# Taking the four batches of a gated recurrence side by side, chunk by chunk

## The chip, the cores and the metric

The kernel runs on one core of one Trainium2 chip, as one launch. The metric is the device time of that launch in microseconds (us), the median of several runs. A profile of one execution is given beside it; its span runs from the first to the last instruction.

## The reference

Two blocks follow each other. The first is a gated linear recurrence (HGRN2) for 4 batches, 8 heads, 768 tokens and 48 channels per head; the second is a feed-forward network on its output, 3072 tokens of 384 channels. Cut to what matters:

```python
f = 1.0 / (1.0 + np.exp(-f_logit))               # (4, 8, 768, 48)
state = np.zeros((B, H, D, D))
for t in range(S):
    state = f[:, :, t, :, None] * state + np.einsum('bhd,bhe->bhde', k[:, :, t], v[:, :, t])
    y[:, :, t] = np.einsum('bhd,bhde->bhe', q[:, :, t], state)
x = y.transpose(0, 2, 1, 3).reshape(B * S, H * D)   # (3072, 384)
h = ((x @ w1) * (x @ w2)) @ w3                      # w1, w2: (384, 1024), w3: (1024, 1024)
out = h @ w_out                                     # (1024, 384)
```

Each batch has its own state, which starts at zero. The four weight matrices arrive as 64-bit floats and are turned into 32-bit ones on the chip.

## The kernel before, in words

**Chunks.** The 4 x 768 tokens are cut into `NU` = 24 chunks of `C` = 128 tokens. Chunk `u` belongs to batch `u // 6`, so chunks 0 to 5 are the first batch in order of time, 6 to 11 the second, and so on. A chunk "opens" when it is the first of its batch (0, 6, 12, 18; no state comes in) and "closes" when it is the last (5, 11, 17, 23; no state goes out). Heads are handled in pairs: a tile has 112 rows, 48 for an even head, 48 for an odd one from row 64 on, and 4 x 128 columns.

**Work of a chunk.** `front` (L477) loads the logits, k, q and v through SyncE's DMA queue (L492, L475), lets ScalarE apply the sigmoid (`gates`, L518) and VectorE run two scans over the gates (`forward`, L526; `backward`, L548); the running products scale q (L542) and k (L556), and the last product of each head is kept in `lasts` (L531). `turning` transposes the scaled k on TensorE (L593) and copies it (L727). `pairs` makes the products of k and q (L569 for chunks 0 and 1, L579 for the others), ScalarE copies them (L700, L703) and GpSimd zeroes what lies above the diagonal (L709). `values` (L653) multiplies the masked products with v, `from_state` (L672) adds q times the state, and `update` (L686) makes the chunk's own contribution to the state. ScalarE writes the result (L845). For chunks 0 and 1 it is brought into the token layout by matmuls (`moved`, L874, and L879); for the others by two DMA writes to DRAM and a DMA read back (L866, L869).

**Two kinds of chunk.** Chunks 0 and 1 (`u < NPE`) are taken whole: `first_values` (L607), four matmuls against the state of the chunk before in a block-diagonal copy (L613; the copy is made by `blocks`, L834), `first_update` (L625) and the state in L822, or L824 and L825. From chunk 2 on a chunk is taken in two halves of 64 tokens: `middle` (L749) makes a state at token 64 (L757 where the chunk opens, else L759 adds the state that comes in) and the state at the end (L762). `state` (L815) multiplies the end state by a gain (L818); the gain is made on GpSimd (`gains`, L809) from `lasts` of this chunk and the first gate of the next one, so it waits for the next chunk's sigmoid.

From chunk 4 on, `visit` (L787) puts the values of chunk `u`, and the pairs and update of chunk `u+1`, into one run of matmuls on TensorE.

**Feed-forward.** Four chunks make a block of 512 tokens (6 blocks). w1 and w2 come in four pieces A, B, C, D (`fetch`, L1378: load L1396, then L1400 on ScalarE and L1415, L1419, L1425 on VectorE); w3 and w_out are folded into one matrix (L1464). Block 0 is multiplied plainly (`part`, L919), blocks 1 and 2 with seven products in place of eight (`seven`, L972), blocks 3 to 5 with a larger scheme of that kind (`many`, L1120). Three of them share the helper `three` at L897. Late in the run ScalarE also looks over the weights' ranges (L1536, L1540), in gaps of its plan.

**Order.** Nothing is scheduled by hand. Each step is a task of a `Plan` (L129) with an engine, an estimated cost, dependencies and a priority; the planner takes at each step the task that can start first by its estimates, then the one with the smaller priority, and the instructions of every engine stand in that order. `need(u)` (L454) is a chunk's due time, 0 to 3 for chunks 0 to 3 and 60 + 14.5 (u - 4) after. `EARLY` (L83) fixes the order of VectorE's early work: chunks 0, 1, 2, 3, then the weight pieces A, C, B, D. Up to the planned time `FULL` = 130, planned gaps of TensorE are filled with matmuls that compute nothing (`idle`, L395, at L399):

```python
    if t["eng"] == "PE" and t["at"] < FULL:
        n = int((t["at"] - ready_at) / 0.43)
        if ready_at and n:
            idle(n)
        ready_at = t["end"]
```

Of the kernel before, what the change touches and what calls it, by code (L numbers as in the profile page):

```python
# [59 lines left out]
NQ = HP * C  # L60
NPE = 2
SOLO = 4
NRAW = 3
# [223 lines left out]


def rows(par):
    return slice(64 * par, 64 * par + D)  # L290
# [3 lines left out]
def ranged(ctx, tc, q, k, f_logit, v, w1, w2, w3, w_out, out, ident, w12, wc, left):  # L294
# [29 lines left out]
    firsts = [keep.tile([P, TB], F32, name=f"a{i}") for i in range(2)]  # L324
    sb = [t[0:R, 0 : HP * R].rearrange("p (h r) -> p h r", r=R) for t in firsts]
    lasts = keep.tile([R, NU, HP], F32, name="lasts")
# [79 lines left out]
    def setup():  # L406
        E = mybir.EngineType
        tc.mark_branch_hint_location("general", hint="LikelyTaken", engines=[E.SP, E.DVE, E.PE, E.Activation, E.Pool])
        nc.scalar.activation(warm, nc.const_aps.tensor(0.0, (R, 1), F32), AF.Sigmoid)
        for i in range(2):  # L410
            if i == 0:
                nc.gpsimd.memset(ks[i][32:64], 0.0)
                nc.gpsimd.memset(qs[i][32:64], 0.0)
                make_identity(nc, ident)
            else:
                nc.gpsimd.memset(fs[i][32:64], 30.0)
        nc.gpsimd.memset(early[32:64, 2:4], 30.0)
# [10 lines left out]
        for t in sb:  # L428
            nc.vector.memset(t, 0.0)
# [43 lines left out]
    def loaded(dst, u):  # L473

        nc.sync.dma_start(dst, v[u])  # L475

    def front(u):  # L477
# [6 lines left out]
        def load(dst, src):  # L484
            def emit():
                if dst is fs[0] and u == 0:

                    nc.sync.dma_start(dst[0:64], src[u].rearrange("two d n -> (two d) n")[0:64])
                    nc.sync.dma_start(dst[rows(1)], src[u, 1])
                    return  # L490
                for par in range(2):
                    nc.sync.dma_start(dst[rows(par)], src[u, par])  # L492
            return emit
# [25 lines left out]

        t["g"] = plan.add("ACT", 0.65, gates, [t["lf"]] + past(u, 2, "r") + past(u, 3, "G"), n0)  # L520
        if u % NCH and "G" in tk[u - 1]:
            tk[u - 1]["G"]["deps"].append(t["g"])

# [74 lines left out]
    def first_values(u):  # L598

        s = st[u]  # L600
        opens = u % NCH == 0
        s["yb"] = bank().rearrange("p (h c) -> p h c", c=C)[0:R]
        for hp in range(HP):
            for par in range(2):
                h = 2 * hp + par
                w = 64 if par == 0 else D
                nc.tensor.matmul(  # L607
                    s["yb"][64 * par : 64 * par + w, hp], lhsT=s["v"][:, h * D : h * D + w],
                    rhs=s["A"][:, par, hp], start=hp == 0, stop=opens, skip_group_check=True,
                )  # L610
        if not opens:
            for hp in range(HP):
                nc.tensor.matmul(  # L613
                    s["yb"][:, hp], lhsT=sb[(u - 1) % 2][:, hp], rhs=s["Q"][:, hp * C : hp * C + C],
                    start=False, stop=True, skip_group_check=True,
                )
# [44 lines left out]
    def from_state(u):  # L661

        s = st[u]
        for half in range(2):
            state = s["mid"] if half else st[u - 1].get("S")
            if state is None or half == 0 and u % NCH == 0:
                continue
# [9 lines left out]
    def update(u):  # L677
# [3 lines left out]
        for hp in range(HP):  # L681
            for half in range(1 if u % NCH == NCH - 1 else 2):
                for par in range(2):
# [37 lines left out]
    def turning(u):  # L721
# [15 lines left out]
    def begin(u):  # L737

        def emit():
# [4 lines left out]
        t["a"] = t["s"] = plan.add(  # L744
            "PE", 1.1, emit, [t["q"], t["k"], t["e"], t["lv"]] + past(u, 1, "m", "d"), need(u) - 999, slack=0.8,
        )
        paired(u)

    def middle(u):  # L749

        s, t = st[u], tk[u]
        opens, closes = u % NCH == 0, u % NCH == NCH - 1

        def emit():
            s["mid"] = mids[u % 2]
            if opens:
                nc.vector.tensor_copy(s["mid"], s["pd"][0])  # L757
            else:
                nc.vector.tensor_tensor(s["mid"], s["pd"][0], st[u - 1]["S"], ALU.add)  # L759
            if not closes:  # L760
                s["S"] = work.tile([R, HP, D], F32, name="S")
                nc.vector.tensor_tensor(s["S"], s["pd"][1], s["mid"], ALU.add)  # L762

        t["mid"] = plan.add(
            "DVE", 0.36 if closes else 0.72, emit, [t["s"], t["m"]] + ([] if opens else past(u, 1, "d")) + past(u, 2, "v"), need(u) - 5,
        )

    def rest(u):
        s, t = st[u], tk[u]
        opens, closes = u % NCH == 0, u % NCH == NCH - 1  # L770
        n0 = need(u)
        if u < NPE:
# [4 lines left out]
            t["v"] = plan.add(  # L777
                "PE", 1.05 if opens else 2.1, lambda: first_values(u), [t["c"], t["lv"]] + past(u, 1, "b"), n0 - 998,
                takes=["f"],
            )  # L780
            t["s"] = plan.add("PE", 0.6, lambda: first_update(u), [t["e"], t["lv"]] + past(u, 1, "d"), n0 - 997)
        else:
# [4 lines left out]
            def visit():  # L787
# [18 lines left out]
        if not closes:  # L806
            def gains():
                s["G"] = work.tile([R, HP], F32, name="G")
                nc.gpsimd.tensor_tensor(s["G"], lasts[:, u], heads(gate[(u + 1) % 2][:, 0:NQ])[:, :, 0], ALU.mult)  # L809

            t["G"] = plan.add(
                "POOL", 0.3, gains, [t["l"]] + [tk[u + 1][nm] for nm in "g" if nm in tk[u + 1]] + past(u, 2, "d"), n0,
            )

            def state():  # L815
                gain = s["G"].unsqueeze(2).to_broadcast([R, HP, D])
                if u >= NPE:
                    nc.vector.tensor_tensor(s["S"], s["S"], gain, ALU.mult)  # L818
                    return
                s["S"] = work.tile([R, HP, D], F32, name="S")  # L820
                if opens:
                    nc.vector.tensor_tensor(s["S"], s["pd"], gain, ALU.mult)  # L822
                else:
                    nc.vector.tensor_tensor(s["S"], s["pd"], st[u - 1]["S"], ALU.add)  # L824
                    nc.vector.tensor_tensor(s["S"], s["S"], gain, ALU.mult)  # L825

            t["d"] = plan.add(
                "DVE", 0.36 if opens or u >= NPE else 0.72, state,
                [t["s"], t["G"]] + (past(u, 2, "b") if u < NPE else [t["mid"]]), n0, shared=True,
            )  # L830

            def blocks():
                for par in range(2):
                    nc.scalar.copy(sb[u % 2][rows(par), :, 64 * par : 64 * par + D], s["S"][rows(par)])  # L834

            if u + 1 < NPE:
                t["b"] = plan.add("ACT", 0.75, blocks, [t["d"]] + past(u, 1, "v"), n0)

# [22 lines left out]
        def written():  # L861

            s["yt"] = dram.tile([DM, C], F32, name="yt")
            for half in range(2):
                to = s["yt"][half * DH : half * DH + DH].rearrange("(b d) c -> d b c", d=D)
                nc.sync.dma_start(to, s["ys"][rows(half)])  # L866

# [13 lines left out]
        before = blk[n - 2]["up"] if n >= 2 else []  # L881
        if u < NPE:
            t["z"] = plan.add("PE", 1.6, moved, [t["y"]], n0 - 996, takes=["f"], frees=[moving])
# [18 lines left out]
    def ffn(n):  # L902
# [329 lines left out]
        def down(i):  # L1232
# [778 lines left out]
```

## Time and profile before

| what | us |
|---|---|
| median of 3 runs | 462.83 (462.68 to 463.16) |
| the profiled execution's own time | 464.25 |
| its span | 462.5 |
| TensorE (PE) busy, mean granted clock | 452.9, 1.000 |
| weight loads (PEld) busy | 395.5 |
| VectorE (DVE) busy | 362.1 |
| ScalarE (ACT) busy | 208.6 |
| GpSimd (POOL) busy | 63.9 |
| DMA moved | 68.75 MB, mean 149 GB/s |

A row of the profile names a line of the program, an engine, an operation and the tiles (out<-in), then how often it ran and how long; "idle before" is the time for which its engine had nothing to do just ahead of it, with what ended that. A 32-bit matmul shows as two passes, that is two records. The chain is the work that ended last, followed back from the last instruction. PE is TensorE's matmul, PEld its weight load, SPq SyncE's queue, which issues the DMAs. Rows of the FFN's start show the buffers by their tile's name: `w` is w1 and w2 as 32-bit floats, `place` a work area for raw weights and temporaries, `xt` the activations of a block, `A` the tile of the masked products, which also holds the states at token 64.

### The profile page before, as it was taken

Reading aid. Unit: us, or ns where it says so; the run is one execution under the profiler, and the core shown is the slowest. Engines: PE = TensorE matmul, PEld = TensorE weight load, DVE = VectorE, ACT = ScalarE, POOL = GpSimd, SP = SyncE. Lnnn points to the kernel's source line nnn. Section 1 sums busy time; section 2 is a strip of 40 time slices with the busy share of each in tenths; the row PEclk is TensorE's granted clock in tenths of the full one; section 3 lists DMA queues with packets and bytes.
Section 4 is the critical chain, followed back from the end, with each engine's and each line's share of the span. In section 5 each row is a group of like instructions: output and inputs, shape, how many; then the busy total and the mean of one; then the engine's idle time right before and its main releaser. Section 6 shows DMA issues by size and latency. Waiting matters only on the chain.

```text
span 462.5 us, 11749 instructions
## 1 busy us (share of the span) xinstructions
PE 452.9 (98%) x4800; PEld 395.5 (86%) x4800; DVE 362.1 (78%) x633; ACT 208.6 (45%) x468; POOL 63.9 (14%) x90
## 2 busy tenths in 40 slices
PE   7999999999999999999999999999999999999995
PEld 6788885666899888888998888998898988889995
DVE  8988899999898999988973599885658566768441
ACT  4565343432233553443323356566675666672000
POOL 9330000211223432223222000000000000000000
PEclk9999999999999999999999999999999999999999
DMA  6896997833246764447324337653265523200111
GB/s 181 272 331 206 336 353 254 267 104 103 70 125 178 213 185 125 111 124 191 102 55 114 112 94 216 201 157 125 95 184 170 192 69 96 89 1 0 35 69 39
DMA packets 43309, 68.75 MB, mean 149 GB/s; under 512 B 5217, under 2 KB 28386, under 8 KB 42226
## 3 DMA queue, kind: packets, MB, share of 16 engines
q1 hardware_dynamic: 43250, 67.95, 47.8%
q8 instruction: 39, 0.64, 0.6%
q14 instruction: 20, 0.16, 0.1%
HBM read 58.88 MB, written 9.04 MB: 147 GB/s over the span
## 4 chain that ended last, share of the span: by engine, by line
PE 94%; POOL 2%; DVE 2%; issue 0%; POOLq 0%; DVEq 0%
PE f L897 25%; PE f L993 15%; PE f L1148 11%; PE f L1464 9%; PE py L1148 6%; PE pa L1148 5%; PE py L897 4%; PE pa L897 4%; PE py L653 3%; PE pa L579 2%; PE pa L686 2%; PE f L593 2%; PE py L672 2%; PE py L993 1%; POOL ab L437 1%; PE f L399 1%
## 5 line engine op out<-in xcount | busy, mean ns | idle before, releaser
L709 POOL TENSOR_SCALAR_AFFINE_SELECT A<-A 64x512 f32<-64x512 f32 (+1 forms) x46 | 42.3, 920 | 110.6 <-ACT A L703 108.5
L1464 PE MATMUL f<-place 128*128 128x384 f32 x128 | 42.4, 487 | 0.0
L897 PE MATMUL f<-xt,w 128*128 128x256 f32 x192 | 42.1, 380 | 0.0
L897 PEld LDWEIGHTS f<-xt,w 128*128 128x128 f32 x192 | 36.3, 190 | 5.0
L1464 PEld LDWEIGHTS f<-place 128*128 128x128 f32 x128 | 23.9, 190 | 15.5
L993 PE MATMUL f<-xt,w 128*128 128x256 f32 x140 | 36.2, 380 | 0.0
L897 PE MATMUL f<-place 128*128 128x192 f32 x192 | 34.8, 327 | 0.0
L897 PEld LDWEIGHTS f<-place 128*128 128x128 f32 x192 | 31.5, 190 | 0.3 <-issue 0.2
L548 DVE TENSOR_TENSOR_SCAN bwd<-gate,back 112x512 f32<-112x512 f32 x24 | 30.4, 1268 | 0.7
L526 DVE TENSOR_TENSOR_SCAN fwd<-gate,floor 112x512 f32<-112x512 f32 x24 | 30.0, 1251 | 1.2 <-ACT gate L518 0.3
L993 PEld LDWEIGHTS f<-xt,w 128*128 128x128 f32 x140 | 26.3, 190 | 3.5
L845 ACT ACTIVATE ys<-py 112x512 f32<-112x512 f32 x22 | 13.1, 596 | 32.7 <-PE py L672 28.1
L1400 ACT ACTIVATE place<-place 128x512 f32<-128x512 uint32 (+2 forms) x24 | 21.3, 888 | 9.1 <-DMA place<-in_w_dram 7.9
L897 PE MATMUL f<-wc,ab 128*128 128x192 f32 x128 | 23.6, 328 | 0.0
L993 PE MATMUL f<-place 128*128 128x256 f32 x84 | 22.4, 385 | 0.0
L897 PEld LDWEIGHTS f<-wc,ab 128*128 128x128 f32 x128 | 21.3, 190 | 0.4
L518 ACT ACTIVATE gate<-f 112x512 f32<-112x512 f32 x22 | 13.9, 632 | 17.0 <-DMA f<-in_f_logit_dram 7.9
L809 POOL TENSOR_TENSOR G<-lasts,gate 112x4 f32<-112x4 f32 x20 | 11.0, 549 | 76.4 <-ACT lasts L531 30.4
L653 PEld LDWEIGHTS py<-A,vt 64*64 64x64 f32 (+1 forms) x672 | 13.3, 127 | 7.3 <-issue 6.5
L653 PE MATMUL py<-A,vt 64*64 64x64 f32 (+1 forms) x672 | 18.1, 223 | 0.2
L1540 ACT ACTIVATE A<-A,back 128x512 f32<-128x512 f32 x23 | 17.9, 778 | 0.2
L1262 DVE TENSOR_TENSOR place<-ab 128x512 f32<-128x512 f32 x24 | 16.5, 689 | 1.0 <-PE f L897 0.9
(355 smaller groups left out, 1045.6 us busy)
## 6 DMA issues: line engine op xcount, KB each, us to landing
place<-in_w_dram SPq DMA_DIRECT2D x21, 512.0 KB, 6.1
A<-in_w_dram SPq DMA_DIRECT2D x19, 512.0 KB, 4.1
place<-in_w_dram SPq DMA_DIRECT2D x8, 1024.0 KB, 5.9
q<-in_q_dram SPq DMA_DIRECT2D x46, 96.0 KB, 2.6
vt<-in_v_dram SPq DMA_DIRECT2D x23, 192.0 KB, 3.1
out_dram<-o SPq DMA_DIRECT2D x23, 192.0 KB, 2.1
k<-in_k_dram SPq DMA_DIRECT2D x44, 96.0 KB, 2.4
yt<-ys SPq DMA_DIRECT2D x44, 96.0 KB, 2.9
```

The lines of the kernel that those rows point to most:

```text
L518: nc.scalar.activation(gate[u % 2][:, 0:NQ], fu, AF.Sigmoid)
L526: nc.vector.tensor_tensor_scan(s["P"], gate[u % 2][:, 0:NQ], floor, 0.0, ALU.mult, ALU.max)
L548: nc.vector.tensor_tensor_scan(s["R"][:, ::-1], gate[u % 2][:, NQ:0:-1], back[:, ::-1], 0.0, ALU.mult, ALU.max)
L653: done = nc.tensor.matmul(y_block(u, hp, par, half)[p0 : p0 + w], lhsT=s["v"][half * W : half * W + W, h * D : h * D + w], rhs=s["A"][half ...
L709: nc.gpsimd.affine_select(out=a, in_=a, pattern=pattern, compare_op=ALU.is_ge, fill=0.0, base=0, channel_multiplier=-1,)
L897: nc.tensor.matmul(out_, lhsT=lhs[i], rhs=rhs[i], start=start and i == 0, stop=i == len(lhs) - 1, skip_group_check=True,)
L993: nc.tensor.matmul(q[nm][:, which * TH : which * TH + TH], lhsT=lhs[i](which), rhs=rhs[i], start=start and which == 0 and i == 0, stop=i = ...
L1148: nc.tensor.matmul(banks[g, c][:, which * TH : which * TH + TH], lhsT=lhs, rhs=x_node(a), start=first and which == 0, stop=True, skip_grou ...
L1262: nc.vector.tensor_tensor(abs_[j], x, y, op)
L1400: nc.scalar.activation(part_.bitcast(F32), part_, AF.Copy, bias=2.0, scale=2.0**-51)
L1464: nc.tensor.matmul(w3s["p", jc], lhsT=w3s[jc][:, kc * P : kc * P + P], rhs=wos[:, kc], start=(kc == 0), stop=(kc == KF - 1),)
L1540: return lambda: nc.scalar.activation(a, a, AF.Sign, bias=small, accum_out=counts[:, i : i + 1])
```

## The change

Chunk `u` now belongs to batch `u % 4`: the data of chunk `u` are found at `chunk(u)`, and the stores of the output go to the matching rows. So chunks 0 to 3 open, 20 to 23 close, and the state that chunk `u` reads is that of chunk `u - 4`; a block holds one chunk of each batch. States wait longer, so they lie in five fixed buffers, three of their own and two in the free columns of the tile `A`. The gain of chunk `u` is made from the first gate of chunk `u + 4`; the gain and the scaling carry the due time of chunk `u + 4`. Chunks 0 and 1 copy their state from PSUM on ScalarE (`saved`) and scale it later like all others; the block-diagonal copies with their memsets, and the four matmuls that read them, are gone. Chunks 2 and 3 stay of the second kind, with a state at token 64, although nothing comes in. Several dependencies name another step: the pairs of a chunk wait for the middle of the chunk before and not for its scaling, the visit for the scaling of chunk `u - 4`.

```diff
+MOVED = 2
...
+def chunk(u):
+
+    return u % B * NCH + u // B
...
-    sb = [t[0:R, 0 : HP * R].rearrange("p (h r) -> p h r", r=R) for t in firsts]
+    states = [keep.tile([R, HP, D], F32, name=f"S{i}") for i in range(3)]
+    states += [t[0:R, 2 * HP * W + HP * D : 2 * HP * W + 2 * HP * D].rearrange("p (h d) -> p h d", d=D) for t in flat]
...
-        nc.sync.dma_start(dst, v[u])
+        nc.sync.dma_start(dst, v[chunk(u)])
...
-                    nc.sync.dma_start(dst[rows(par)], src[u, par])
+                    nc.sync.dma_start(dst[rows(par)], src[chunk(u), par])
...
-        t["g"] = plan.add("ACT", 0.65, gates, [t["lf"]] + past(u, 2, "r") + past(u, 3, "G"), n0)
-        if u % NCH and "G" in tk[u - 1]:
-            tk[u - 1]["G"]["deps"].append(t["g"])
+        t["g"] = plan.add("ACT", 0.65, gates, [t["lf"]] + past(u, 2, "r") + past(u, B + 2, "G"), n0)
+        if u >= B and "G" in tk[u - B]:
+            tk[u - B]["G"]["deps"].append(t["g"])
...
-        if not opens:
-            for hp in range(HP):
-                nc.tensor.matmul(
-                    s["yb"][:, hp], lhsT=sb[(u - 1) % 2][:, hp], rhs=s["Q"][:, hp * C : hp * C + C],
-                    start=False, stop=True, skip_group_check=True,
-                )
...
-            state = s["mid"] if half else st[u - 1].get("S")
-            if state is None or half == 0 and u % NCH == 0:
+            state = s["mid"] if half else st[u - B]["S"] if u >= B else None
+            if state is None:
...
-            for half in range(1 if u % NCH == NCH - 1 else 2):
+            for half in range(1 if u + B >= NU else 2):
...
-            t["t"] = plan.add("PE", 0.45, lambda: turn(u), [t["k"]] + past(u, 1, "d"), need(u) - 999)
+            t["t"] = plan.add("PE", 0.45, lambda: turn(u), [t["k"]] + past(u, 1, "sc"), need(u) - 999)
...
-            "PE", 1.1, emit, [t["q"], t["k"], t["e"], t["lv"]] + past(u, 1, "m", "d"), need(u) - 999, slack=0.8,
+            "PE", 1.1, emit, [t["q"], t["k"], t["e"], t["lv"]] + past(u, 1, "m", "mid"), need(u) - 999, slack=0.8,
...
-        opens, closes = u % NCH == 0, u % NCH == NCH - 1
+        opens, closes = u < B, u + B >= NU
...
-                nc.vector.tensor_tensor(s["mid"], s["pd"][0], st[u - 1]["S"], ALU.add)
+                nc.vector.tensor_tensor(s["mid"], s["pd"][0], st[u - B]["S"], ALU.add)
             if not closes:
-                s["S"] = work.tile([R, HP, D], F32, name="S")
+                s["S"] = states[u % len(states)]
...
-            "DVE", 0.36 if closes else 0.72, emit, [t["s"], t["m"]] + ([] if opens else past(u, 1, "d")) + past(u, 2, "v"), need(u) - 5,
+            "DVE", 0.36 if closes else 0.72, emit, [t["s"], t["m"]] + past(u, B, "d") + past(u, 1, "v") + past(u, 2, "v"), need(u) - 5,
...
-                [t["c"], t["lv"], t["mid"]] + past(u, 1, "y", *([] if opens else ["d"])) + [after[nm] for nm in ("q", "k", "e", "lv") if after],
+                [t["c"], t["lv"], t["mid"]] + past(u, 1, "y", "sc") + past(u, B, "d") + [after[nm] for nm in ("q", "k", "e", "lv") if after],
...
-                nc.gpsimd.tensor_tensor(s["G"], lasts[:, u], heads(gate[(u + 1) % 2][:, 0:NQ])[:, :, 0], ALU.mult)
+                nc.gpsimd.tensor_tensor(s["G"], lasts[:, u], heads(gate[(u + B) % 2][:, 0:NQ])[:, :, 0], ALU.mult)
...
+            if u < NPE:
+                def saved():
+                    s["S"] = states[u % len(states)]
+                    nc.scalar.copy(s["S"], s["pd"])
+
+                t["sc"] = plan.add("ACT", 0.33, saved, [t["s"]] + past(u, 1, "v"), n0)
...
+                nc.vector.tensor_tensor(s["S"], s["S"], s["G"].unsqueeze(2).to_broadcast([R, HP, D]), ALU.mult)
+
+            t["d"] = plan.add("DVE", 0.36, state, [t["G"], t["sc" if u < NPE else "mid"]], need(u + B) if u + B < NU else n0, shared=True)
...
-                    t0 = n * TB + (i + half * UB // 2) * P
+                    t0 = ((i + half * UB // 2) * NCH + n) * P
```

More of the change, by code (lines that the diff above doesn't have):

```diff
@@ L427, in setup @@
         nc.vector.memset(qs[1][32:64], 0.0)
-        for t in sb:
-            nc.vector.memset(t, 0.0)
         nc.gpsimd.memset(perm, 0.0)
@@ L486, in emit @@
                 if dst is fs[0] and u == 0:
-                    nc.sync.dma_start(dst[0:64], src[u].rearrange("two d n -> (two d) n")[0:64])
-                    nc.sync.dma_start(dst[rows(1)], src[u, 1])
+                    nc.sync.dma_start(dst[0:64], src[chunk(u)].rearrange("two d n -> (two d) n")[0:64])
+                    nc.sync.dma_start(dst[rows(1)], src[chunk(u), 1])
                     return
                 for par in range(2):
-                    nc.sync.dma_start(dst[rows(par)], src[u, par])
+                    nc.sync.dma_start(dst[rows(par)], src[chunk(u), par])
             return emit
@@ L600, in first_values @@
         s = st[u]
-        opens = u % NCH == 0
         s["yb"] = bank().rearrange("p (h c) -> p h c", c=C)[0:R]
@@ L608, in first_values @@
                     s["yb"][64 * par : 64 * par + w, hp], lhsT=s["v"][:, h * D : h * D + w],
-                    rhs=s["A"][:, par, hp], start=hp == 0, stop=opens, skip_group_check=True,
-                )
-        if not opens:
-            for hp in range(HP):
-                nc.tensor.matmul(
-                    s["yb"][:, hp], lhsT=sb[(u - 1) % 2][:, hp], rhs=s["Q"][:, hp * C : hp * C + C],
-                    start=False, stop=True, skip_group_check=True,
+                    rhs=s["A"][:, par, hp], start=hp == 0, stop=True, skip_group_check=True,
                 )
@@ L769, in rest @@
         s, t = st[u], tk[u]
-        opens, closes = u % NCH == 0, u % NCH == NCH - 1
+        opens, closes = u < B, u + B >= NU
         n0 = need(u)
@@ L777, in rest @@
             t["v"] = plan.add(
-                "PE", 1.05 if opens else 2.1, lambda: first_values(u), [t["c"], t["lv"]] + past(u, 1, "b"), n0 - 998,
+                "PE", 1.05, lambda: first_values(u), [t["c"], t["lv"]], n0 - 998,
                 takes=["f"],
             )
-            t["s"] = plan.add("PE", 0.6, lambda: first_update(u), [t["e"], t["lv"]] + past(u, 1, "d"), n0 - 997)
+            t["s"] = plan.add("PE", 0.6, lambda: first_update(u), [t["e"], t["lv"]] + past(u, 1, "sc"), n0 - 997)
         else:
@@ L808, in gains @@
                 s["G"] = work.tile([R, HP], F32, name="G")
-                nc.gpsimd.tensor_tensor(s["G"], lasts[:, u], heads(gate[(u + 1) % 2][:, 0:NQ])[:, :, 0], ALU.mult)
+                nc.gpsimd.tensor_tensor(s["G"], lasts[:, u], heads(gate[(u + B) % 2][:, 0:NQ])[:, :, 0], ALU.mult)
             t["G"] = plan.add(
-                "POOL", 0.3, gains, [t["l"]] + [tk[u + 1][nm] for nm in "g" if nm in tk[u + 1]] + past(u, 2, "d"), n0,
+                "POOL", 0.3, gains, [t["l"]] + past(u, 2, "d"), need(u + B) if u + B < NU else n0,
             )
-            def state():
[L816 to L837, printed above, removed]
+            if u < NPE:
[3 more added lines that the diff above has]
+                t["sc"] = plan.add("ACT", 0.33, saved, [t["s"]] + past(u, 1, "v"), n0)
+            def state():
+                nc.vector.tensor_tensor(s["S"], s["S"], s["G"].unsqueeze(2).to_broadcast([R, HP, D]), ALU.mult)
+            t["d"] = plan.add("DVE", 0.36, state, [t["G"], t["sc" if u < NPE else "mid"]], need(u + B) if u + B < NU else n0, shared=True)
         def outcome():
@@ L865, in written @@
                 to = s["yt"][half * DH : half * DH + DH].rearrange("(b d) c -> d b c", d=D)
+                if u < NPE:
+                    to = s["yt"].rearrange("(b two d) c -> two d b c", two=2, d=D)[half]
                 nc.sync.dma_start(to, s["ys"][rows(half)])
@@ L881, in rest @@
         before = blk[n - 2]["up"] if n >= 2 else []
-        if u < NPE:
+        if u < MOVED:
             t["z"] = plan.add("PE", 1.6, moved, [t["y"]], n0 - 996, takes=["f"], frees=[moving])
```

## The prediction

> **What bounds the kernel now.** I read the page's busy line first, then the busy time by stretch, then the chain that ended last in order of time, then the start of the run instruction by instruction.
>
> The page's first part, for the whole span:
>
> ```profile
> span 462.5 us, 11749 instructions
> PE 452.9 (98%) x4800; PEld 395.5 (86%) x4800; DVE 362.1 (78%) x633; ACT 208.6 (45%) x468; POOL 63.9 (14%) x90
> ```
>
> TensorE has 9.6 us without a matmul in 462.5. The table of stretches (stretch and its length, then busy us of PE, PEld, DVE, ACT and POOL, then clock, DMA share, GB/s) says where:
>
> ```profile
> 20.00:30.00 10.00, 9.78 (x242) 8.60 (x243) 9.16 (x13) 6.32 (x14) 1.95 (x2) 1.00 0.93 348
> 30.00:41.00 11.00, 10.90 (x109) 9.28 (x108) 9.86 (x8) 7.01 (x15) 1.91 (x2) 1.00 0.95 308
> 68.00:118.00 50.00, 50.00 (x535) 31.61 (x537) 47.29 (x61) 18.44 (x34) 6.97 (x9) 1.00 0.58 180
> 151.00:264.00 113.00, 112.78 (x2092) 100.57 (x2091) 91.89 (x163) 43.89 (x105) 28.07 (x36) 1.00 0.48 135
> 264.00:457.00 193.00, 192.43 (x1002) 177.23 (x1000) 133.75 (x275) 102.02 (x237) 0.00 (x0) 1.00 0.35 108
> ```
>
> After 30 us PE is never without work for longer than a few tenths. Busy matmul time alone would be weak evidence, so I checked the pace: in the chain, 132 passes of the up projection lie in 28.49 us, 0.216 us each, with no gap, and the same 0.216 returns at 388.04 (28 passes in 6.04 us). So from 30.6 to 457.3 us the time is the sum of PE's work, and a shorter recurrence is worth only what PE waits for it. The chain before that point (start, length, what):
>
> ```profile
> 11.74 0.18 POOL G L809
> 11.94 0.06 DVE S L822
> 12.21 1.27 DVE K L556
> 20.08 1.08 PE f L607 x16
> 21.16 1.06 PE f L613 x8
> 25.17 1.73 PE f L399 x8
> 29.55 1.06 PE f L399 x4
> 30.61 3.89 PE f L897 x18
> ```
>
> The reader is to see two things: chunk 0's gain and state (L809, L822) stand in the chain, and L399, which computes nothing (the program fills gaps it plans with these), fills the last wait before the first real FFN product at 30.6. What that product waits for is in VectorE's timeline (start, length, line, out<-in):
>
> ```profile
> 22.96 0.68 DVE L542 TENSOR_TENSOR Q<-place,fwd 112x512 f32<-112x512 f32 x1
> 23.89 0.96 DVE L1415 TENSOR_SCALAR place<-place 128x1536 uint32<-128x1536 uint32 x1 [0.25 <-DMA place<-in_w_dram]
> 24.77 0.35 DVE L759 TENSOR_TENSOR A<-pa,S 112x192 f32<-112x192 f32 x1
> 25.15 0.36 DVE L762 TENSOR_TENSOR S<-pa,A 112x192 f32<-112x192 f32 x1
> 25.61 0.68 DVE L818 TENSOR_TENSOR S<-S,G 112x192 f32<-112x192 f32 x1
> 26.21 1.75 DVE L1419 SCALAR_TENSOR_TENSOR w<-place 128x1536 uint32<-128x1536 uint32 x1
> 27.99 1.76 DVE L1425 CUSTOM_DVE_ANT_0 w<-place,w 128x3072 uint16<-128x3072 uint16 x1
> ```
>
> The first weight piece A (w1, first half) is converted by L1415, L1419, L1425. Its data arrive at 23.85, and between its first and second step VectorE does chunk 2's state at token 64 (L759), its end state (L762) and its gain (L818).
>
> [...] (a pass is booked at 0.38 us and starts every 0.216), which is why I use the pace. [...] the gain L818 took 0.68 us while GpSimd's mask L709 ran (24.07 to 26.08), 0.36 us at 45.98 without it. [...] the v load at 27.91 waited 4.1 us for a matmul of L653, and the weight load at 28.28 came right behind it.
>
> **The change, part by part.**
>
> *PE's work.* Removed: the four matmuls of chunk 1 against chunk 0's state, L613, 1.06 us, but before 30.6. A half chunk's product with a state (L672) is 32 passes in 0.45 us for two halves, 0.225 each. Chunks 2 and 3 lose one half each, chunk 3's after 30.6; chunks 6, 12 and 18, which open a batch now, gain one each. After 30.6: (3 - 1) x 0.225 = **+0.45 us**. The second half of the update (L686) is left out for chunks 20 to 23 in place of 5, 11, 17, 23: sum 0, but 5, 11 and 17 carry it earlier.
>
> *VectorE, start.* Removed: two memsets of 0.91 together (hidden: the first scan waits for the gate until 4.72), L822 with its wait (11.72 to 12.21: 0.49), L824 and L825 (20.38 to 21.10: 0.72). So chunk 3's Q could end at 23.64 - 1.21 = 22.4. That alone is worth nothing: A's data still land at 23.85. What counts is behind it. L818 for chunk 2 moves to the time of chunk 6; and the pairs of chunk 2 (22.15) stood behind L613 and waited for chunk 1's L825, so they come 1.06 us or more earlier. Their copy (ended 24.01) is then ready by 22.95, and L759 and L762 (0.72 us) fit in front of 23.89. L1419 follows L1415 at 24.85 and not at 26.21: **A is joined 1.36 us earlier**, at 28.4. ScalarE's third piece of A (L1400, 24.34 to 25.06) must then be done by 24.85; it sits behind two copies of the same chunks that also come 1.06 earlier, so I cost it at 0 (if not, 0.2 us).
>
> *New copies on ScalarE.* Chunks 0 and 1 copy their state from PSUM. The trace has no such row; nearest are L727 (0.54 for 448 columns) and L531 (0.20 for 4), so 0.2 to 0.54 for 192 columns: I take 0.33 each. The two block copies (0.71 in all) go. Behind them wait chunk 1's transposes, at 15.32, which wait for K (13.48) anyway: 0, at most +0.3 if K is also early.
>
> *Gains and scaling, moved.* The gain of chunk u now waits for the gate of chunk u+4, the scaling follows, and chunk u+4's middle state waits for the scaling. Behind a late gain on GpSimd stands a mask; who waits is that chunk's visit on PE. But before, the gain of u-1 waited for the same gate, so the queue waits as long: 0. From 45 to 118 us VectorE had L818 for chunks 3, 4, 6; it now has four, and chunk 5's end state: 0.40 + 0.36 = +0.76 us on an engine 47.29/50 busy. The fold it feeds has slack (the last converted row of w3 is ready at 106.5, used at 111.7), so 0; with that cover gone up to 1.3, with GpSimd in the way.
>
> *Moved DMA.* Loads and stores have the same sizes at other addresses: 0. Their issue on SyncE moves: the v load behind L607 (21.19) and behind chunk 2's visit (27.91) each hold weight loads. If the visit comes 1 us earlier, so do they, but at 93 to 95% DMA share only part is gained.
>
> *The order.* The planner sorts every task again. Idle left to win is 0.22 us (151 to 264) and 0.57 (264 to 457); to lose, I allow 2 us (some delayed copies at 0.6 each). I take 0.
>
> *Does 1.36 survive?* Piece C was joined at 36.03 and used at 37.2; with PE at 35.8 it must come 0.2 earlier, and chunk 3's middle state, between its steps (0.64), can move ahead. B: 40.81 against 42.4, slack 1.6. Chunk 3's activations landed at 47.6, just as PE turned to them; they must come 1.4 earlier, which they do if its visit (34.42) moves with the rest. The fold's operand was ready at 67.25 for 68.44, with 24 up passes (5.38 us, at 118.6) as reserve. So I let it pass whole.
>
> **Sum**: -1.36 + 0.45 = -0.91 us. The profiled execution took 464.25 us (span 462.5 and 1.75 around it), so 463.34; it lay 1.42 above the median of the runs, so against 462.83: **461.9 us**.
>
> **Rivals.**
> 1. *More is won*: the first product stood 0.69 us behind A's join because PE was in L399; without that, and without the 0.86 us of L399 at 123.98, -1.36 - 0.69 - 0.86 + 0.45 = -2.46: 460.4. For it: the visits of chunks 2 and 3 no longer wait on a state. Against: C then comes late (only 1.2 us of slack).
> 2. *The start is held by DMA*: loads that are issued earlier share bandwidth with A, or chunk 3's activations still land at 47.6. Then only the extra work stays: +0.45, 463.3. For it: 93% DMA share.
> 3. *Slower: SyncE's queue.* If the new order puts the pairs and update of chunk 3 (0.64 + 0.62 as booked, some 1.3) ahead of chunk 2's visit, the v load waits that much longer, and behind it B's second piece, chunk 2's activations and D. B slips from 40.81 to 42.1, still hidden; chunk 3's activations slip past 47.6 and PE waits 1.3. With +0.45: +1.75, 464.6; with a slip half as large again (1.95), 465.2. It decides from a visit of chunk 2 that starts later than 26.83 + 0.5. Against: the visit's own inputs come earlier.
> 4. *It doesn't do what it says* can be left out: the state's reader changes in every chunk.
>
> **How the numbers follow.** Forecast 0.42 (461.2 to 462.7); rival 1 0.18; rival 2 0.15; rival 3, with other delays of the new order, 0.25. A measurement here can tell some 0.2% (0.93 us) from none: faster means below 461.9, slower above 463.76. The forecast lies on the edge: 0.27 of its 0.42 goes to faster, 0.15 to same; with rival 1 faster is 0.45. Rival 2 gives 0.12 to same and 0.03 to slower: same 0.27, slower 0.28. Range 460.0 to 465.3, from rival 1 with half of the 0.79 us of idle won too, to rival 3 with the larger slip; the likeliest case's own is above.
>
> **What would show it.** L613 gone; L759 of chunk 2 ahead of the first L1415; L1419 at about 24.9 and the first L897 at 29.1; no gap in PE between 40 and 68; 320 in place of 304 passes of L672 that read an earlier chunk's state (20 chunks of 16, not 19). I am wrong if A's join doesn't move, if PE waits at about 46 us, or if the gaps after 118 us grow past 1.4 us.

## The result, and the profile after

The changed kernel took **465.93 us** in the median of six runs (465.48 to 466.62) against 462.83 of the kernel before (six runs as well): ratio 1.0065 with an interval of 1.0054 to 1.0076, about 3 us slower. The forecast was 461.9. The profiled execution took 466.02 us with a span of 464.3. A ratio, here and below, is to runs of the kernel before that were made beside the run; their median lay between 462.8 and 463.5 us.

Where lines are named below, those of the kernel after are meant. They answer to those of before so: L885 to L897 (`three`), L981 to L993 (`seven`), L1136 to L1148 (a product of `many`), L1157 to L1169 (a copy of such a product), L1022 to L1034 (a copy in `seven`), L1180 to L1192 and L1250 to L1262 (sums on VectorE), L406 to L399, L547 to L542, L651 to L653, L670 to L672, L755 to L757 and L760 to L762, L1403, L1407, L1413 to L1415, L1419, L1425, and L1524, L1528 to L1536, L1540. In kernels of the experiments with added lines they are shifted by a few.

The page's first part, of the kernel after:

```profile
span 464.3 us, 11737 instructions
...
PE 452.5 (97%) x4804; PEld 392.9 (85%) x4804; DVE 359.3 (77%) x630; ACT 207.0 (45%) x468; POOL 66.5 (14%) x90
```

TensorE is booked as busy for as long as before (452.9), in a span that is 1.8 us longer, so the time is not extra work: it stands still more. The stretches, with the columns of before:

```profile
20.00:30.00 10.00, 8.55 (x212) 7.15 (x209) 9.08 (x12) 6.18 (x14) 4.24 (x4) 1.00 0.92 309
...
151.00:264.00 113.00, 112.90 (x2107) 100.79 (x2107) 90.61 (x165) 43.86 (x106) 28.59 (x39) 1.00 0.48 132
264.00:457.00 193.00, 191.10 (x984) 173.65 (x984) 134.34 (x275) 101.30 (x237) 0.00 (x0) 1.00 0.35 110
```

Two of these stretches differ. From 20 to 30 us PE now stands for 1.45 us (0.22 before), and from 264 to 457 us, where the last chunk is done and only FFN products are left (the third stage below), for 1.90 (0.57 before). (From 10 to 20 us PE is also busy for less, 8.53 us in place of 9.39; that lies ahead of the wait for piece A, which the next part is about.) The middle, in which the chunks from 4 on are worked, has no new idle: 0.10 us from 151 to 264, 0.22 before, and none from 68 to 151 in either. So the recurrence itself, which the change is about, runs as well as before.

**The start.** The chain at the start of the kernel after (start, length, what):

```profile
26.68 0.84 PE f L406 x3
27.52 1.35 issue
28.87 1.35 PE f L406 x5
30.22 2.59 PE f L885 x12
```

And VectorE's timeline just before:

```profile
22.55 1.14 DVE L547 TENSOR_TENSOR Q<-place,fwd 112x512 f32<-112x512 f32 x1
23.61 0.34 DVE L755 COPY A<-pa 112x192 f32<-112x192 f32 x1
23.99 0.36 DVE L760 TENSOR_TENSOR S<-pa,A 112x192 f32<-112x192 f32 x1
24.27 0.95 DVE L1403 TENSOR_SCALAR place<-place 128x1536 uint32<-128x1536 uint32 x1
25.13 1.76 DVE L1407 SCALAR_TENSOR_TENSOR w<-place 128x1536 uint32<-128x1536 uint32 x1
26.93 1.76 DVE L1413 CUSTOM_DVE_ANT_0 w<-place,w 128x3072 uint16<-128x3072 uint16 x1
```

Chunk 2's middle and end state (L755, L760) stand ahead of the first weight step, and the gain is gone from between the steps, as forecast. Piece A is joined at 26.93 + 1.76 = 28.69 (29.75 before). Yet the first up product ran at 30.22 (30.61 before): PE stood for 1.35 us between two filling matmuls, for nothing that the profile shows ("issue"), while A was ready. The last experiment asks whether that stop is part of the kernel.

**The end.** From 264 us on, the chain of before leaves PE once (353.06 to 355.30) ahead of its last sum; the pieces that are not PE there:

```profile
353.15 0.70 DVE a L1192
...
354.60 0.70 DVE ys L1192
...
457.30 0.36 DVE o L1313
```

The one wait of PE that its trace lists in that stretch is

```profile
PE py L897 <- DVE ys L1192: 0.6, 1, 0.6
```

The chain of after leaves PE five times. The main of its pieces that are not PE, in order of time:

```profile
278.14 0.58 ACT Q L1157
278.72 0.65 ACT A L1524 x2
279.38 0.48 ACT place L1022
...
337.97 0.60 ACT place L1157
...
380.14 0.60 ACT ys L1157
...
405.04 0.60 ACT a L1157
...
426.38 0.59 ACT ys L1157
...
426.99 0.70 DVE Q L1180
```

The waits of PE in that stretch of after (line, waited for, us, times, longest) are four of these:

```profile
PE pa L1136 <- ACT place L1022: 0.9, 1, 0.9
PE py L1136 <- ACT place L1157: 0.3, 1, 0.3
PE pa L1136 <- ACT ys L1157: 0.3, 1, 0.3
PE pa L1136 <- ACT a L1157: 0.3, 1, 0.3
```

Every one is a product that waits for ScalarE to copy another product out of its tile. That makes 1.8 us as booked. By the pace it is more: four passes that start at 404.36 last until 405.22 at 0.2158 us each, and the next product starts at 405.69, so that stop is 0.47 and not 0.30; a group of passes behind a stop also lasts 0.10 us longer (1.13 for four passes in place of 1.03). Counted so (1.10 at 278, 0.47 at each of the three places that follow, 0.23 at 429.87, and 0.10 behind each), the five places cost 1.20 + 3 x 0.57 + 0.33 = 3.2 us; the one of before 0.74 + 0.10.

**Why the copy is late.** ScalarE's timeline of after at the fourth place:

```profile
401.03 0.58 ACT L1157 COPY place<-pa 128x512 f32<-128x512 f32 x1 [0.47 <-PE pa L1136]
...
404.56 0.59 ACT L1157 COPY Q<-pa 128x512 f32<-128x512 f32 x1 [2.19 <-PE pa L1136]
405.04 0.59 ACT L1157 COPY a<-pa 128x512 f32<-128x512 f32 x1
```

And PE's:

```profile
402.64 1.03 PE L1136 MATMUL pa<-place,floor 128*128 128x256 f32 x4
403.50 1.03 PE L1136 MATMUL pa<-xt,w 128*128 128x256 f32 x4
404.36 1.03 PE L1136 MATMUL py<-xt,gate 128*128 128x256 f32 x4
405.69 1.13 PE L1136 MATMUL pa<-place,Q 128*128 128x256 f32 x4 [0.30 <-ACT a L1157]
```

The first row is the product that the copy into Q takes; it ends at 402.64 + 1.03 = 403.67. ScalarE is idle, and still the copy starts at 404.56, after the second row has ended (404.53). That second product has nothing to do with the copy, except for where it lies. In the third stage four banks of PSUM are shared, and the kernel before makes them in this way as well:

```python
nm = ("pa", "py")[(plan.got - NF) // 2]
if nm not in found:
    found[nm] = ps.tile([P, 2, NQ], F32, name=nm)
return found[nm][:, plan.got % 2]
```

`pa` and `py` are tiles of two banks each, and a half is handed out as if it were a bank of its own. In the program as built, a read of one half waits for the product that was written last to the tile, whichever half it went to. If a second product stands between a product and its copy on PE and goes to the other half, the copy waits for it too: it is **held**.

It goes the other way as well: a product waits for the last read of its tile, whichever half that took. The fourth product above goes to the half that the copy into Q empties (with one-bank tiles, below, both stand under the name `pa_x`). That copy ended at 404.56 + 0.59 = 405.15, before PE was through with the third product (405.22). The product started at 405.69, just after the copy into `a` had ended (405.63), and that copy is out of the other half. So the held copy brings two copies together, and the product, held in its turn, waits for the second of them. At all four places of the list, the wait in the program as built names the copy out of the other half.

The expectations below speak of held copies and sums: 3 in the kernel before, 10 in the kernel after. No trace shows this count. By the waits of the two programs as built it is 11 and 13 reads whose wait names a later product in the other half, and of ScalarE's copies alone 2 and 8. None of the third stage's work was changed; the planner only put it in another order.

### The profile page after: what moved, and what is told of

Same layout as the page of the kernel before. It is cut to its first block, busy times and chain, and to the rows that moved or that the text cites. A ratio compares the mean times of both kernels' runs of the same rounds, so it can differ in the third digit from the quotient of the medians.

```text
span 464.3 us, 11737 instructions
## 1 busy us (share of the span) xinstructions
PE 452.5 (97%) x4804; PEld 392.9 (85%) x4804; DVE 359.3 (77%) x630; ACT 207.0 (45%) x468; POOL 66.5 (14%) x90
## 4 chain that ended last, share of the span: by engine, by line
PE 94%; SPq 1%; DVE 1%; issue 1%; ACT 1%; DMA 1%; POOL 0%; POOLq 0%
PE f L885 25%; PE f L981 15%; PE f L1136 9%; PE f L1452 9%; PE py L1136 7%; PE pa L1136 5%; PE pa L885 4%; PE py L651 3%; PE py L885 2%; PE pa L584 2%; PE pa L684 2%; PE f L598 2%; PE py L670 2%; PE pa L981 1%; PE f L406 1%
## 5 line engine op out<-in xcount | busy, mean ns | idle before, releaser
L707 POOL TENSOR_SCALAR_AFFINE_SELECT A<-A 64x512 f32<-64x512 f32 (+1 forms) x46 | 45.6, 991 | 102.5 <-ACT A L701 96.5
L885 PE MATMUL f<-xt,w 128*128 128x256 f32 x192 | 42.4, 381 | 0.0
L885 PEld LDWEIGHTS f<-xt,w 128*128 128x128 f32 x192 | 36.1, 190 | 5.1 <-issue 0.2
L885 PE MATMUL f<-place 128*128 128x192 f32 x208 | 38.1, 327 | 0.0
L1452 PEld LDWEIGHTS f<-place 128*128 128x128 f32 x128 | 23.9, 190 | 15.5
L981 PE MATMUL f<-xt,w 128*128 128x256 f32 x140 | 35.7, 380 | 0.0
L885 PEld LDWEIGHTS f<-place 128*128 128x128 f32 x208 | 34.2, 190 | 0.4 <-issue 0.2
L981 PEld LDWEIGHTS f<-xt,w 128*128 128x128 f32 x140 | 26.4, 190 | 3.5
L885 PE MATMUL f<-wc,ab 128*128 128x192 f32 x128 | 23.4, 326 | 0.0
L981 PE MATMUL f<-place 128*128 128x256 f32 x84 | 22.4, 385 | 0.0
L885 PEld LDWEIGHTS f<-wc,ab 128*128 128x128 f32 x128 | 21.4, 190 | 0.4
L651 PEld LDWEIGHTS py<-A,vt 64*64 64x64 f32 (+1 forms) x672 | 13.3, 127 | 7.1 <-issue 6.3
L651 PE MATMUL py<-A,vt 64*64 64x64 f32 (+1 forms) x672 | 18.0, 223 | 0.2
L1528 ACT ACTIVATE A<-A,back 128x512 f32<-128x512 f32 x23 | 18.0, 781 | 0.2
L547 DVE TENSOR_TENSOR Q<-q,fwd 112x512 f32<-112x512 f32 x23 | 17.5, 762 | 0.0
```

The source lines that it names most:

```text
L547: nc.vector.tensor_tensor(s["Q"], qu, s["P"], ALU.mult)
L651: done = nc.tensor.matmul(y_block(u, hp, par, half)[p0 : p0 + w], lhsT=s["v"][half * W : half * W + W, h * D : h * D + w], rhs=s["A"][half ...
L707: nc.gpsimd.affine_select(out=a, in_=a, pattern=pattern, compare_op=ALU.is_ge, fill=0.0, base=0, channel_multiplier=-1,)
L885: nc.tensor.matmul(out_, lhsT=lhs[i], rhs=rhs[i], start=start and i == 0, stop=i == len(lhs) - 1, skip_group_check=True,)
L981: nc.tensor.matmul(q[nm][:, which * TH : which * TH + TH], lhsT=lhs[i](which), rhs=rhs[i], start=start and which == 0 and i == 0, stop=i = ...
L1452: nc.tensor.matmul(w3s["p", jc], lhsT=w3s[jc][:, kc * P : kc * P + P], rhs=wos[:, kc], start=(kc == 0), stop=(kc == KF - 1),)
```

## The experiments

Theory 1, formed before the first four runs: the time is lost by the order of the third stage. Rivals: another cause in the third stage (the looks over the ranges, L1524, which stand in the chain at 278), or the start.

**The tails exchanged.** The kernel after, whose last 753 steps (those planned from 258 us on) are put into the sequence, and into the banks, in which the kernel before has them; and the reverse. The instructions are the same, only the order of the end is given by hand:

```diff
-    for t in plan.order():
+    listed = plan.order()
+    by_no = {t["no"]: t for t in listed}
+    del listed[CUT:]
+    for word in TAIL.split():
+        no, _, got = word.partition(":")
+        listed.append(by_no[int(no)])
+        if got:
+            by_no[int(no)]["got"] = int(got)
+    for t in listed:
```

> The changed kernel, but from planned time 258 (after the last chunk's visit) its 753 remaining steps stand in the sequence of the kernel before, with that kernel's choice of PSUM banks. Theory 1 (the new sequence of the feed-forward steps after 264 us makes PE wait for ScalarE's copies): the loss of 2.7 us of feed-forward progress after 264 us goes, the time is 462.7 to 463.4, and PE has one gap like that at 353 us before and no others. Theory 2 (the changed attention itself costs time: more state work, longer-lived states): nothing changes, 465.5 to 466.5.

Measured: 462.93 us, ratio 0.9982 (0.9969 to 0.9995). The part of its chain that isn't PE, from 262 us on, is that of before, 1.4 us earlier (353.15 and 457.30 there):

```profile
351.74 0.70 DVE a L1184
...
352.47 0.70 DVE ys L1184
...
455.89 0.36 DVE o L1305
```

> The converse: the kernel before, with its last 747 steps in the sequence and with the banks of the changed one. Theory 1: it becomes slower by the same 2.4 to 3 us, 465.2 to 466.0, with gaps near 278, 337, 380, 404 and 426 us. Theory 2: no change, 462.6 to 463.2.

Measured: 466.63 us, ratio 1.0067 (1.0044 to 1.0091), with stops of PE for the same four copies as in the kernel after. So the order of the end, with the banks that go with it, is worth the whole loss, in either kernel; and with it put right the change is a small gain.

**Short looks.** The kernel after, in which a look over the weights' ranges reads 8 columns in place of 512 (it leaves out most of that test):

```diff
-        his = [t.rearrange("p (n two) -> p n two", two=2)[:, :, 1].bitcast(F32) for t in words]
+        his = [t.rearrange("p (n two) -> p n two", two=2)[:, 0:8, 1].bitcast(F32) for t in words]
```

> The changed kernel, its order untouched, with ScalarE's 68 passes over the weights' ranges made 64 times shorter (8 columns of 512 are looked at, so most of the range check is left out). If the looks that stand in front of copies make the gaps (theory 3), PE's waits after 264 us go and the time is 462.5 to 463.5. If the gaps come from products that reopen a bank whose copy has just begun (theory 1 in its narrow form), only the gap at 278 us, where a look of 0.65 us stands between two copies, shrinks: 465.0 to 465.6.

Measured: 465.53 us, ratio 1.0037 (1.0024 to 1.0051). PE's waits of that run from 264 us on:

```profile
PE pa L1136 <- ACT place L1022: 0.5, 1, 0.5
...
```

The other three waits are those of after, 0.3 us each. A look that sits between two late copies adds 0.4 us at 278 and nothing at the other places. It makes one stop longer, and causes none. By the two ratios (1.0037 and 1.0065) this kernel is some 1.3 us faster than the kernel after; the trace shows 0.4 of that, and where the rest lies is not shown.

**No filling ahead of the first product.** The kernel after without the four matmuls of L406 that fill the wait for piece A:

```diff
-            if ready_at and n:
+            if ready_at and n and not 26.0 < ready_at < 28.0:
```

> The changed kernel without the four fill matmuls (8 passes, 1.73 us) that stand ahead of the first up product. Piece A is joined at 28.69 and the first product starts at 30.05. If the fill holds it, it starts at 28.9 to 29.2 and, should the lead survive, the time falls by about 1 us, to 464.9. If the lead is lost again because piece C (joined at 35.48) or chunk 3's activations come no earlier, the first product moves and the time doesn't: 465.6 to 466.2.

Measured: 466.45 us, ratio 1.0051 (1.0038 to 1.0063); nothing is won. The first product did start at 29.01, but its 12 passes took 4.54 us, 0.378 each on average:

```profile
29.01 4.54 PE L885 MATMUL f<-xt,w 128*128 128x256 f32 x12 [2.06 <-DVE w L1413]
```

The stretches of this run (the column after POOL is the granted clock):

```profile
28.00:30.00 2.00, 0.99 (x4) 0.91 (x5) 1.58 (x3) 1.06 (x2) 1.94 (x2) 0.94 1.01 332
30.00:32.00 2.00, 2.00 (x6) 1.55 (x6) 1.61 (x2) 1.07 (x2) 0.19 (x1) 0.50 0.93 337
32.00:34.00 2.00, 1.93 (x21) 1.22 (x19) 1.97 (x2) 0.37 (x1) 0.00 (x0) 0.71 1.00 338
```

PE had stood for 2.06 us, and 0.75 us later it went to half clock for some 3.4 us (the last section works this out). With the filling, in the runs without the 1.35 us stop, the first product starts as early (28.8 to 29.05 us). So the filling matmuls hold nothing up, and with them the granted clock was 1.00 from 28 to 34 us, in the kernel after and in the one with the tail of before. In this run the first down pass (the first product with the matrix folded from w3 and w_out) started at 125.1 us, some 1.1 us later than in those runs. In the whole time the difference to the kernel after is not clear of noise.

**One tile for each bank.** Theory 2, from the timelines above: it is the held copies. The kernels after and before with no instruction moved, but in the third stage with four tiles of one bank in place of two tiles of two:

```diff
-            nm = ("pa", "py")[(plan.got - NF) // 2]
-            if nm not in found:
-                found[nm] = ps.tile([P, 2, NQ], F32, name=nm)
-            return found[nm][:, plan.got % 2]
+            if "split" not in found:
+                ps_open.close()
+                found["split"] = ctx.enter_context(tc.tile_pool(name="ps_s", bufs=1, space=PSUM))
+            if ("b", plan.got) not in found:
+                nm = ("pa", "py")[(plan.got - NF) // 2] + "_" + "xz"[plan.got % 2]
+                found["b", plan.got] = found["split"].tile([P, NQ], F32, name=nm)
+            return found["b", plan.got]
```

> The changed kernel with every instruction in its place; in the third stage each of the four shared banks of PSUM is a tile of its own (before: two tiles of two banks each, so that a copy out of one half also stands behind a product that was queued into the other half meanwhile; 10 copies and sums of the third stage do so in the changed kernel, 3 in the kernel before). Theory (the lost time is those held copies): the gaps of TensorE near 337, 380, 404 and 426 us go (1.10, 1.10, 1.10 and 3.47 us in the chain of the changed kernel), and that near 278 loses the part that isn't the two looks; ratio to before 0.995 to 0.9995. Rival (the order itself is worse: the copies are late because ScalarE has other work ahead of them): the gaps stay, ratio 1.004 to 1.0075. In between (1.000 to 1.004): both.

Measured: **461.81 us, ratio 0.9959** (0.9944 to 0.9973). ScalarE's timeline at the same place of the sequence as above:

```profile
397.73 0.59 ACT L1161 COPY place<-pa_x 128x512 f32<-128x512 f32 x1 [0.47 <-PE pa_x L1140]
...
400.32 0.59 ACT L1161 COPY Q<-pa_x 128x512 f32<-128x512 f32 x1 [1.24 <-PE pa_x L1140]
401.18 0.59 ACT L1161 COPY a<-pa_z 128x512 f32<-128x512 f32 x1 [0.28 <-PE pa_z L1140]
```

PE's timeline there:

```profile
399.25 1.03 PE L1140 MATMUL pa_x<-place,floor 128*128 128x256 f32 x4
400.12 1.03 PE L1140 MATMUL pa_z<-xt,w 128*128 128x256 f32 x4
400.98 1.03 PE L1140 MATMUL py_z<-xt,gate 128*128 128x256 f32 x4
401.85 1.03 PE L1140 MATMUL pa_x<-place,Q 128*128 128x256 f32 x4
```

The products are those of after, in the same order. The copy into Q now starts as its own product ends (400.28), the two copies lie 0.86 us apart and not back to back, and the fourth product follows 0.87 us behind the third, at full pace. All five stops are gone. From 264 us to the end PE waits for nothing; the stretch in this kernel is

```profile
264.00:455.00 191.00, 191.00 (x996) 176.79 (x995) 134.90 (x276) 102.42 (x237) 0.00 (x0) 1.00 0.34 111
```

At the place of the first stop the look still stands between two copies (276.34 us here) and delays nothing: it lay in the chain because the copy ahead of it was held, and the product behind it waited for the copy out of the other half. This edit takes away both kinds of wait at once, that of the copies and that of the products; no run parts the two.

> The kernel before with the same edit: four tiles of one bank in place of two tiles of two in the third stage, every instruction in its place. Theory: its only gap of the third stage (353.06 to 355.30 us in the chain, 2.24 us, of which the three rows of VectorE stand) goes in part, ratio 0.996 to 0.999. Rival (the held copies cost nothing here): 0.9995 to 1.0005.

Measured: 462.58 us, ratio 0.9981 (0.9967 to 0.9995). The only stop of before goes as well. With both kernels freed of held copies, the change alone is worth 0.9959 / 0.9981 = 0.9978, some 1 us less; the two intervals taken together leave 0.9958 to 0.9998, that is 0.1 to 1.9 us.

**Both at once.** The kernel after with the tail of before and one-bank tiles.

> The changed kernel up to about 258 us, then the sequence of the kernel before, and one-bank tiles. Theory: the lead of the start (0.6 to 0.8 us in the run without the new tiles) and the gain of the tiles add up, ratio 0.994 to 0.998, the fastest of all. Rival: the lead or the tiles' gain is met by another wait, ratio 0.998 to 1.000.

Measured: 461.99 us, ratio 0.9970 (0.9959 to 0.9980), not to be told from the kernel after with one-bank tiles alone (spans 460.1 and 460.2). Without held copies the order of the tail doesn't matter: in both, PE has no wait from 264 us on. That this would be the fastest of all was not borne out, since there was nothing left to add up.

**Another re-sort.** The kernel before with a planner's number changed, so that the third stage is sorted otherwise, with 6 held copies and sums:

```diff
-BEGIN = 0.6
+BEGIN = 0.3
```

> The kernel before with one number of the planner changed that has nothing to do with the chunks: it takes TensorE as free 0.3 us later than the first load in place of 0.6, so that it sorts the third stage otherwise; 6 copies and sums stand behind a product of the other half of their tile in place of 3. Theory (a re-sorted tail costs by the number and the place of held copies, whatever re-sorts it): slower by 0.3 to 2 us, ratio 1.0005 to 1.004. Rival (only the order of the chunks makes the tail worse): 0.9995 to 1.0005.

Measured: 463.76 us, ratio 1.0006 (0.9991 to 1.0021): it decides nothing. The profile shows one wait of PE there, 0.3 us for a copy. The new order costs at most 1 us here, so the number of held copies alone is no measure: one can cost only where a product soon wants the tile or the result.

**One tile of four banks.** The kernel before, its order kept, with the four shared banks as one tile of four:

```diff
-            nm = ("pa", "py")[(plan.got - NF) // 2]
-            if nm not in found:
-                found[nm] = ps.tile([P, 2, NQ], F32, name=nm)
-            return found[nm][:, plan.got % 2]
+            if "four" not in found:
+                found["four"] = found["split"].tile([P, 4, NQ], F32, name="pq")
+            return found["four"][:, plan.got - NF]
```

> The kernel before, every instruction in its place, but in the third stage the four shared banks are one tile of four, so that a copy or sum out of one bank stands behind a product queued meanwhile into any of the other three: 26 copies and sums do so in place of 3. Theory: in the changed kernel seven more of them cost some 3.5 us, 0.5 us each; 23 more cost 3 to 12 us, ratio 1.006 to 1.026, with gaps of TensorE at the copies after the products with many. Rival (it was the places in the sequence, and the held copies only went along): 0.9995 to 1.002.

Measured: 480.51 us, **ratio 1.0351** (1.0306 to 1.0396), more than I gave it: 17.5 us. That is 0.76 us for each of the 23 more held reads of the expectation, but no price of a held read, since products are held by this tile as well. The longest of PE's waits from 264 us on:

```profile
PE pq L1151 <- ACT ys L1172: 2.3, 4, 1.2
PE pq L1151 <- ACT a L1172: 1.8, 2, 1.5
PE pq L996 <- ACT A L1543: 1.5, 1, 1.5
```

Most of the stops are of the kind seen in the kernel after, a product behind a copy or a sum; the third row names a look (L1543, which is L1540 of before). The order of the work was untouched, so the tile alone makes them.

**The start once more.** The kernel after, profiled a second time.

> The changed kernel once more, for its start. In its first profile TensorE stood 1.35 us ahead of the first up product for nothing that the profile shows, and that product ran at 30.05 us; in the profiles of three runs that are the same program up to there it ran at 28.8 to 29.0 us. If the stop belongs to that one execution: first up product at 28.7 to 29.1 us here. If it belongs to the program: 29.9 to 30.2 us.

Measured: 465.82 us in its one run. L885's first group in this profile (count: ns min/median/max, first and last start):

```profile
L885 PE MATMUL f<-xt,w x192: 379/379/483, 29.0 to 122.9; 128*128 128x256 f32 x192
```

The first product ran at 29.0 us, so the stop of 1.35 us belongs to the one execution. It is no part of the loss: this run was no faster for it.

## Why the prediction was wrong

**The step that failed** is "The order": "to lose, I allow 2 us (some delayed copies at 0.6 each). I take 0." It was not 0 but 3 to 4 us: in the kernel before, the other order of the end added 3.1 us (466.63, against 463.50 of before in the runs beside it); between the kernel after and the same with the tail of before, the two ratios leave 3.8. The exchange of tails moves the loss with the order (0.9982 and 1.0067), and the one-bank tiles take it away with the order as it is (0.9959). So the loss needs both: a new order, and tiles of two banks under which an order can be bad. The delayed copies that I allowed for were the right kind of event, and their price was near (0.6; 0.57 at three of the places). But I gave no reason for taking none, and put the term at 0. There was something to go by: the kernel before had a stop of that kind in its chain (353.06 to 355.30), which went with the tiles, and `bank` hands out halves of a tile. Once seen, any re-sort of the third stage would have been a risk to one side only, since before had 0.57 us of idle to win.

**A's join 1.36 us earlier** was right in its mechanism and near in size: L818 is gone from between the steps and chunk 2's states went ahead of them. The join came 1.06 us earlier (28.69). The missing 0.3 is chunk 3's Q (L547): the first weight step started at 24.27, behind it, and not at 23.89. I had Q end at 22.4; it ended at 23.69. It began only 0.41 us earlier than before, where I had counted 1.21, and it took 1.14 us in place of 0.68, with GpSimd masking meanwhile (L707, 22.30 to 24.21).

**Two more matmul groups, +0.45 us**, is borne out in the count. L670 has, in the kernel after,

```profile
L670 PE MATMUL py<-Q,A 48*48 48x64 f32 x480 | 10.7, 216 | 0.0
L670 PE MATMUL py<-Q,S 48*48 48x64 f32 x192 | 4.9, 215 | 0.0
```

672 passes. The tile `A` holds the states at token 64, which 352 passes read as before, and now also some of the chunks' states: 480 - 352 + 192 = 320 passes read an earlier chunk's state, where before 304 did.

**Does 1.36 survive?** What there was of it, 1.06, does in the main. In five profiles of the changed start without the 1.35 us stop and with the filling kept (the runs with the tail of before, short looks, one-bank tiles, both, and the repeat) the first down pass starts at 123.2, 124.3, 124.0, 123.9 and 124.0 us; in those with the start of before (itself, one-bank tiles, the re-sort, the tail of after, one tile of four) at 124.7, 124.9, 124.9, 125.0 and 125.9. The medians, 124.0 and 124.9, are 0.9 us apart. The forecast for this point is 1.36, since the two matmul groups come behind it (chunk 3's is won and chunk 6's lost ahead of it; those of chunks 12 and 18 follow). In the profiles of the two kernels with one-bank tiles (after and before) the last sum starts at 455.71 and 456.25, so 0.54 us are left at the end, against the sum of 0.91; their runs say 1 us, 0.1 to 1.9. So the sum had the right sign and form for what it counted, and was if anything too large.

**The rivals.** More won: no, the filling at 26.7 us did not hold the first product; in the profiled execution without it the granted clock was 0.50 from 30 to 32 us, against 1.00 with it. Start held by DMA: no, A came earlier, though in the run with one-bank tiles PE stood 0.7 us in all for later inputs of the up products, before 124 us. SyncE's queue: no, chunk 2's visit (its first matmul, L651) ran at 24.53 and not at 26.83, so nothing stood ahead of it, and PE had no stop near 46 us. Its chance was meant to hold "other delays of the new order" too, and it is these that came; but the mechanism that I named for the slower side was another, and its upper end of 465.2 us, which set the range, fell short of 465.93.

**What would show it wrong**: of the three signs I gave, the third came. The gaps after 118 us were 0.79 us before and are 0.10 + 1.90 = 2.00 after.

Left open: why PE stood for 1.35 us in one execution, and what each of the two kinds of wait would cost alone. From the first down pass (124.4 and 124.0 us) to the last sum (460.07 and 455.71) the kernel after takes 335.6 us, and 331.7 with one-bank tiles. Of these 3.9 us, 3.2 lie in the five stops. Another 0.64 lie in eight places of the third stage at which a product into `pa` or `py` starts 0.08 us late (in the chain, four passes at 383.64 and at 408.55 take 0.95 and 0.94 us in place of 0.86); with one-bank tiles none of the eight is left.

## What to carry to other kernels

When a planner or a compiler sorts all work again, a change at the start can be paid for at the end; put the tail of the old order under the new kernel, and see whether the loss goes with it. In this kernel a wait was as coarse as the tile that it was kept for: with two banks to a tile the copy into Q started 0.89 us after its product had ended (404.56 against 403.67), with one bank 0.04 us after (400.32 against 400.28). So two buffers that are handed out separately should be separate tiles, or, as here, a reader of one also waits for the last writer of the other, and a writer for the last reader. In the trace this showed as a copy that started late on an idle engine, as the next product into the same tile ended (404.53); look for it before costing a new order at nothing.

## What the runs showed of the hardware

In the profiled execution without the filling, TensorE stood for 2.06 us (to 29.01), and 0.75 us after it had begun again its granted clock was down to half. With the clock read as either full or half, the mean of 0.94 from 28 to 30 us is a full clock until about 29.76 and half of it after, and that of 0.71 from 32 to 34 puts the end of the half clock at about 33.16: 3.4 us, an estimate from the two means; from 30 to 32 us the clock was 0.50. The passes agree: of the 12 behind the stop, the eight that start from 29.76 to 32.75 lie 0.427 us apart, about twice the 0.216 of elsewhere. With the filling the clock was 1.00 from 28 to 34 us, in the profile of the kernel after, where TensorE stood for 1.35 us until 28.87, and in that of the run with the tail of before.

Half clock for 3.4 us takes some 0.004 off the mean of a run of 465 us. Of the 22 runs without the filling, 15 have a mean granted clock of 0.994 to 0.996, the profiled one (0.994) among them, and seven one of 0.999 or 1.000; the six runs of the kernel after have 0.998 to 1.000. So the drop is not in every execution without the filling, and one profile does not show from what length of a stop on it comes.
